# A fused attention and gated MLP on one core: six small moves in an order written out by hand

## The chip, the cores and the metric

The kernel runs on one core of one Trainium2 chip. The time is the device time of one execution in microseconds. The profile is that of one execution; all times inside it count from the start of its span.

## What is computed

Two branches read the same x (2048 rows of 1024) and are mixed by a gate of each row:

```
qkv = x @ wqkv                                  # 32 heads of 32
o   = softmax(q . k over 8 rows, 2 apart) @ v   # only rows s, s-2, ... s-14
a   = o @ wo
z   = gelu(x @ w_in);  z1, z2 = z[:, :1792], layernorm(z[:, 1792:])
g   = w_sp @ z2 + b_sp                          # mixes the 2048 rows
b   = (z1 * g) @ w_out
out = sigmoid((x * gate_w).sum(-1)) * a + (1 - sigmoid(...)) * b
```

## The kernel before

**Stages on TensorE.** (1) From 6 us: the first tiles of z2, each 8 matmuls of 448 columns (`z2_tile`, L351); then group 0 of qkv (`qkv_tile`, L724, 16 tiles of 8 matmuls of 384 columns). (2) Groups 1 to 7 of qkv, with eight z2 tiles after group 1, to 201 us; then the rest of z2. (3) z1 from about 271 us (L825): 64 tiles, each evicted by ScalarE through gelu (L827) into a staging buffer, two of them, of four tiles, stored by SP (L832). (4) The mixing by w_sp, 369 to 540 us: 16 groups `g_group(n)`, each of seven products of eight matmuls of 448 columns (L846). A group is one 2 x 2 step of Winograd's form of Strassen's product: seven products in place of eight, with sums of the operands made beforehand on VectorE (L588 to L593 for the rows of w_sp, L597 for z2), and sums of the results in PSUM, on ScalarE (`fork` L870, `keep` L856 and L858, a cast L891, L901) and on VectorE (`vec` L862). At the end of a group VectorE multiplies by z1 (L902). (5) o @ wo, 540 to about 589 us, in the same way, K of four tiles: `wo_group`, eight of them (u, two row tiles each), taken in pairs, so that product i of u and of u + 1 stand side by side. (6) y @ w_out, eight groups of seven products of 7 matmuls of 512 columns, with the final mix (`finish`, L1014, and L1091 to L1098) and the stores of the output.

The products of (4) to (6) are in f16, so their operands are scaled by powers of two taken from sums of absolute values. Rows of w_sp: L558 sums them on ScalarE, `row_power` (L562 to L565) makes the powers, `row_store` (L570 to L577) transposes them and stores them to DRAM (`rs_d`), `load_scale` (L584) reads them back for a pair of row tiles, spread over all partitions, and `scale_rows` (L588) uses them. The attention output o: `o_norm(g)` (L494) sums a head group of it on ScalarE, `o_total` (L497, L498) adds the groups up, `o_power` has TensorE add over the partitions by one matmul of 8 columns (L503) and VectorE make the powers (L504 to L509), and `heads_sums(u)` (L514 to L518) scales the rows of o for wo_group u, once `load_heads` has brought them transposed, and makes their sums. `w_scale(b)` (L985, four instructions each) scales half b of w_out.

**Attention** runs on VectorE beside stages (2) to (4): `attention_steps` yields pieces (L374 to L414) for eight head groups; ScalarE does the exponentials (L392).

**What sets the order.** The whole program is under a manual schedule: instructions stand on each engine in the order in which the Python code issues them. `Beat` keeps a planned clock: `beat.run(cols)` moves it by the columns that TensorE has been given, and issues what is due; `beat.at(t, fn)` plans fn for the time t; `vector_steps` issues attention's pieces whenever VectorE, by its own planned time, would be free. In the mixing stage three more lists are served at fixed places of a group: `beside_fork` (after L884, one entry if due), `beside_copy` (after L891, one entry if due) and `behind_mult` (after L902, entries with a planned cost, as many as fit a room of 5.0 us, of 7.4 from group 13 on). When attention is done, `attended` plans what follows, relative to the planned time t at that point: the loads of o for pairs 0 and 1, `o_total` from t + 4 on, `o_power` from t + 12 on, the scaling of wo, and `heads_sums(0)`, all by `behind_mult`; `heads_sums(1)` is appended to that list after group 13 with no earliest time.

## Time and profile before

| what | before |
|---|---|
| median of 3 runs | 678.3 us (677.97 to 679.02) |
| the profiled execution | 679.4 us |
| its span | 677.6 us |
| TensorE busy | 670.0 us (99%) |
| VectorE busy | 550.5 us (81%) |
| ScalarE busy | 394.1 us (58%) |
| granted TensorE clock | 1.00 |
| last product starts, last matmul ends | 672.45, 673.97 us |

The span runs from the first instruction to the last; the execution's time has some 1.8 us around it. PE is the matrix engine (PEld its weight loads), DVE is VectorE, ACT is ScalarE, SP the engine that issues most of the transfers; a q behind a name means the engine's instruction queue, not its unit. In the waits, "PE ps L825 <- ACT arena L827: 0.7, 1, 0.7" reads: TensorE's instructions of line 825 that write the tile ps waited for ScalarE's L827, 0.7 us in all, once, 0.7 at the longest. In the chain each line is a start, a duration and who did it, in order of time. In the timelines a line is a start, a duration, the engine, line and operation, output <- input and shapes, and in brackets the idle time just before and who ended it.

### The profile page before, as it was taken

The numbers are of one execution on the slowest core, as the hardware profiler recorded it, in microseconds if no ns is written. First come the engines' busy times: TensorE is split into PE (matmuls) and PEld (weight loads), VectorE is DVE, ScalarE is ACT, GpSimd is POOL, SyncE is SP. The second block draws the span as 40 slices with busy tenths as digits, with TensorE's granted clock in tenths as the row PEclk, the third lists the DMA queues.
The fourth block names the chain that finished last, engine by engine and source line by source line (L and its number), as shares of the span: only waits on it lengthen the run. The fifth ranks groups of instructions, "written<-read, shape, count | busy, mean of one in ns | idle before, by whom it ended". The sixth has DMA issues, their size and how long they took to land.

```text
span 677.6 us, 9538 instructions
## 1 busy us (share of the span) xinstructions
PE 670.0 (99%) x3590; PEld 392.5 (58%) x3590; DVE 550.5 (81%) x628; ACT 394.1 (58%) x736; POOL 13.1 (2%) x23
## 2 busy tenths in 40 slices
PE   9999999999999999999999999999999999999997
PEld 4577788888885555554555554555555544444443
DVE  1009799999999999999999999999957996944745
ACT  4445657565645988855983557566564664522121
POOL 1000000000000000013100000000000000000000
PEclk9999999999999999999999999999999999999999
DMA  9989769989769760527674857395769699485211
GB/s 232 178 223 236 214 176 276 239 193 270 169 170 278 266 214 3 198 73 211 231 233 137 183 135 187 108 283 133 189 208 242 128 252 252 93 177 145 58 63 62
DMA packets 230734, 123.92 MB, mean 183 GB/s; under 512 B 191008, under 2 KB 217248, under 8 KB 230688
## 3 DMA queue, kind: packets, MB, share of 16 engines
q1 hardware_dynamic: 229104, 121.21, 68.2%
q10 hardware_dynamic: 1584, 2.10, 0.9%
q8 instruction: 28, 0.46, 0.3%
q14 instruction: 18, 0.15, 0.1%
HBM read 63.97 MB, written 37.82 MB: 150 GB/s over the span
## 4 chain that ended last, share of the span: by engine, by line
PE 80%; DVE 10%; SPq 3%; DMA 3%; ACT 2%; issue 1%; ACTq 0%; DVEq 0%
PE ps L846 36%; PE ps L724 18%; PE sd L724 6%; PE seed L846 6%; PE ps L825 5%; PE ps L351 5%; DVE arena L407 2%; PE sd L825 2%; PE sd L351 2%; SPq L709 1%; DVE arena L377 1%; DVE arena L374 1%; DMA z_d<-arena 1%; DVE arena L413 1%; DMA arena<-o_d 1%
## 5 line engine op out<-in xcount | busy, mean ns | idle before, releaser
L846 PE MATMUL ps<-arena 128*128 128x448 f16 (+1 forms) x1296 | 264.8, 363 | 1.1 <-DVE arena L1014 0.6
L846 PEld LDWEIGHTS <-arena 128*128 128x128 f16 x1512 | 147.7, 98 | 156.3 <-issue 2.4
L724 PEld LDWEIGHTS <-arena 128*128 128x128 bf16 x1024 | 141.6, 138 | 25.8 <-issue 1.0
L724 PE MATMUL ps<-arena 128*128 128x384 bf16 x768 | 130.4, 326 | 0.6 <-DMA arena<-in_A_wqkv_dram 0.6
L374 DVE TENSOR_TENSOR arena<-arena 128x8192 bf16<-128x8192 bf16 x16 | 70.7, 4420 | 46.0 <-DMA arena<-k_d 45.8
L377 DVE TENSOR_TENSOR arena<-arena 128x4096 bf16<-128x4096 bf16 (+1 forms) x64 | 77.6, 1213 | 2.0
L825 PEld LDWEIGHTS <-arena 128*128 128x128 bf16 x512 | 50.0, 98 | 47.6 <-issue 1.2
L351 PEld LDWEIGHTS <-arena 128*128 128x128 bf16 x512 | 50.1, 98 | 46.7 <-issue 0.2
L351 PE MATMUL ps<-arena 128*128 128x448 bf16 (+1 forms) x384 | 77.0, 353 | 0.0
L825 PE MATMUL ps<-arena 128*128 128x448 bf16 x384 | 75.6, 352 | 0.7 <-ACT arena L827 0.7
L407 DVE TENSOR_TENSOR arena<-arena,att_A 128x8192 bf16<-128x8192 bf16 x16 | 70.7, 4421 | 0.2
L732 ACT CAST arena<-ps 128x384 bf16<-128x384 f32 x84 | 39.3, 483 | 42.3 <-PE ps L724 40.1
L846 PE MATMUL seed<-arena 128*128 128x448 f16 (+1 forms) x216 | 47.8, 363 | 0.0
L724 PE MATMUL sd<-arena 128*128 128x384 bf16 x256 | 46.8, 326 | 0.0
L827 ACT ACTIVATE arena<-ps 128x448 bf16<-128x448 f32 x48 | 24.9, 552 | 24.4 <-PE ps L825 13.7
L357 ACT ACTIVATE arena<-ps 128x448 bf16<-128x448 f32 x48 | 26.2, 550 | 21.5 <-PE ps L351 21.1
L413 DVE TENSOR_TENSOR arena<-arena 128x4096 bf16<-128x4096 bf16 x16 | 36.6, 2290 | 0.4
L1071 ACT ACTIVATE arena<-ps,omr 128x512 f32<-128x512 f32 x24 | 16.5, 688 | 32.7 <-PE ps L846 32.7
L1014 DVE SCALAR_TENSOR_TENSOR arena<-seed,omr,arena 128x512 bf16<-128x512 f32 x8 | 6.0, 751 | 34.5 <-PE seed L846 34.5
L858 ACT ACTIVATE arena<-ps,bt 128x448 f32<-128x448 f32 x32 | 20.3, 634 | 21.9 <-PE ps L846 19.8
L558 ACT ACTIVATE arena<-arena 128x2048 bf16<-128x2048 bf16 x16 | 30.7, 1922 | 0.0
L680 ACT ACTIVATE arena<-arena 128x896 bf16<-128x896 bf16 x32 | 30.2, 945 | 0.5
(144 smaller groups left out, 630.0 us busy)
## 6 DMA issues: line engine op xcount, KB each, us to landing
arena<-in_B_w_sp_dram SPq DMA_DIRECT2D x16, 512.0 KB, 4.7
arena<-k_d SPq DMA_DIRECT2D x8, 960.0 KB, 7.3
arena<-v_d SPq DMA_DIRECT2D x8, 960.0 KB, 5.9
z_d<-arena SPq DMA_DIRECT2D x16, 448.0 KB, 2.7
arena<-z_d SPq DMA_DIRECT2D x16, 448.0 KB, 4.1
y_d<-arena SPq DMA_DIRECT2D x16, 448.0 KB, 3.5
arena<-in_A_wqkv_dram SPq DMA_DIRECT2D x24, 256.0 KB, 5.6
arena<-in_B_w_in_dram SPq DMA_DIRECT2D x6, 896.0 KB, 7.9
```

Source lines behind the costliest of these rows:

```text
L351: nc.tensor.matmul(ps[:, 0:N], xT[:, kt, i * P:(i + 1) * P], w2[:, kt, ZC * c:ZC * c + N], start=(kt == 0), stop=(kt == KT - 1))
L357: nc.scalar.activation(z2[:, i, ZC * c:ZC * (c + 1)], ps[:, 0:ZC], ACT.Gelu_apprx_tanh, accum_out=s1[:, 4 * i + c:4 * i + c + 1])
L374: TT(prod.rearrange("p (w j c) -> p w j c", w=W, j=8, c=C), in0, in1, ALU.mult)
L377: return lambda: TT(pv[:, :, 0:half], pv[:, :, 0:half], pv[:, :, half:2 * half], ALU.add)
L407: TT(prod.rearrange("p (w j d h) -> p w j d h", w=W, j=8, d=DH, h=HG), in0, in1, ALU.mult)
L413: return [(4.4, mul), (2.3, lambda: TT(p3[:, 0:4, :], p3[:, 0:4, :], p3[:, 4:8, :], ALU.add)), (1.2, lambda: TT(p3[:, 0:2, :], p3[:, 0:2, ...
L558: nc.scalar.activation(waste, slot, ACT.Abs, accum_out=l1[:, a:a + 1])
L680: nc.scalar.activation(waste, g_ring[n % 4][:, r], ACT.Abs, accum_out=yl[:, k:k + 1])
L724: nc.tensor.matmul(ps[:, 0:3 * C].rearrange("p (t c) -> p t c", t=3), lhsT, wgt[:, 0:3, kt, :], start=(kt == 0), stop=(kt == KT - 1))
L732: nc.scalar.copy(st[:, j % 4, :], ps[:, 0:3 * C])
L825: nc.tensor.matmul(ps[:, 0:ZC], xT[:, kt, i * P:(i + 1) * P], w1[:, kt, :], start=(kt == 0), stop=(kt == KT - 1))
L846: nc.tensor.matmul(ps[:, 0:c1 - c0], w[:, k, :], v[:, k, c0:c1], start=(first and k == 0), stop=(k == K - 1), skip_group_check=True)
```

## The change

- `store_scale` is split off `row_store`: the store of the row scales (L577) is planned at t + 38 instead of within `row_store` at t + 20, and the first `load_scale` at t + 46 instead of t + 22.
- A tiny Exp on four columns is put into `beside_copy` ahead of the mixing stage, so that it is issued in group 0.
- `o_norm`, planned 17 us after a head group, goes to `beside_fork` if the mixing stage has begun by the time that it is due (`o_norm_soon`).
- `heads_sums(7)` is planned at +20.5 us after the first pair of wo groups instead of +17, and `w_scale(1)` at t + 30 instead of t + 31.
- z2 tile (2, 1) is issued ahead of qkv group 0 instead of after qkv.
- The last product of the last group is issued as two halves of 256 columns, each followed by its `finish` and its store.

```diff
                 else:
-                    beat.at(t + 17.0, lambda g=g: o_norm(g - 1, obuf))
+                    beat.at(t + 17.0, lambda g=g: o_norm_soon(g - 1))
...
+    def o_norm_soon(g):
+        if prep["mixing"]:
+            beside_fork.append((0.0, lambda: o_norm(g, obuf)))
+        else:
+            o_norm(g, obuf)
+
...
         beat.on_vector(0.8)
+
+    def store_scale():
         sync.dma_start(rs_d.rearrange("(a t) -> a t", t=P), rs_r[:])
...
         z2_tile(i, 0)
+    z2_tile(2, 1)
     beat.steps = vector_steps(beat.now + NJ * KT * 3 * C * BEAT + 8.0)
...
     for i in range(16):
-        for c in range(1 if i > 1 else 2, 4):
+        for c in range(1 if i > 2 else 2, 4):
             z2_tile(i, c)
...
     beat.at(t + 20.0, row_store)
-    beat.at(t + 22.0, lambda: load_scale(0))
+    beat.at(t + 38.0, store_scale)
+    beat.at(t + 46.0, lambda: load_scale(0))
...
+    beside_copy.append((0.0, lambda: nc.scalar.activation(wsc[:, 3:4], cm05[:, 0:1], ACT.Exp)))
     for m in range(11):
         beside_copy.append((beat.now + 10.0, lambda m=m: wo_norm(m)))
...
-    beat.at(t + 31.0, lambda: w_scale(1))
+    beat.at(t + 30.0, lambda: w_scale(1))
...
-            plan_heads(7, beat.now + 0.3, 1.5, beat.now + 17.0)
+            plan_heads(7, beat.now + 0.3, 1.5, beat.now + 20.5)
...
-        product(pa, v.a22, e4, 0, 512, False)
-        finish(o21, pa, hi, m21)
         if u == NU - 1:
             sync.dma_start(out2[(2 * u + 1) * P:(2 * u + 2) * P, 512:D], o22)
-            sync.dma_start(out2[(2 * u + 1) * P:(2 * u + 2) * P, 0:512], o21)
+            for c0 in (0, 256):
+                sl = slice(c0, c0 + 256)
+                for k in range(NF // 2):
+                    nc.tensor.matmul(pa[:, sl], v.a22[:, k, :], e4[:, k, sl], start=False,
+                                     stop=(k == NF // 2 - 1), skip_group_check=True)
+                nc.vector.scalar_tensor_tensor(o21[:, sl], pa[:, sl], hi, m21[:, sl], ALU.mult, ALU.add)
+                sync.dma_start(out2[(2 * u + 1) * P:(2 * u + 2) * P, sl], o21[:, sl])
         else:
+            product(pa, v.a22, e4, 0, 512, False)
+            finish(o21, pa, hi, m21)
             sync.dma_start(out2[(2 * u + 1) * P:(2 * u + 2) * P, :], ob_slots[2 * u + 1])
```

## The prediction

> **What bounds the kernel now.** I read the page's first two parts, then the waits of TensorE, then the chain of work that ended last around each of those waits, then the timelines of VectorE and TensorE where the built order of the changed kernel differs.

> ```profile
> PE 670.0 (99%) x3590; PEld 392.5 (58%) x3590; DVE 550.5 (81%) x628; ACT 394.1 (58%) x736; POOL 13.1 (2%) x23
> ...
> PE   9999999999999999999999999999999999999997
> ...
> DVE  1009799999999999999999999999957996944745
> ```

> TensorE is busy for 670.0 of 677.6 us, in every slice. VectorE is nearly full only in the slices up to 500 us. So the end moves only by what stands between two matmuls, and by the tail behind the last one. All such gaps together are small:

> ```profile
> PE ps L825 <- ACT arena L827: 0.7, 1, 0.7
> PE ps L724 <- DMA arena<-in_A_wqkv_dram: 0.6, 1, 0.6
> PE ps L846 <- DVE arena L1014: 0.6, 1, 0.6
> PE ps L846 <- ACT arena L858: 0.5, 1, 0.5
> ```

> These are idle times. Measured from matmul start to matmul start against the usual spacing, the trace gives 0.79 us at 22.08, 0.91 and 0.12 at 321.74 and 326.40, 0.18 at 386.24, 0.64 at 411.10, 0.12 at 547.67, 0.22 at 551.35 and 0.74 at 575.39: 3.72 us. More than this cannot be won ahead of the tail. The chain says what each of them waited for:

> ```profile
> 16.90 5.05 DMA arena<-in_A_wqkv_dram
> ```
> ```profile
> 302.20 4.27 SPq L584
> ...
> 308.57 6.81 DMA z_d<-arena
> ```
> ```profile
> 406.77 1.28 ACT L392
> ```
> ```profile
> 564.22 5.63 DMA arena<-o_d
> ...
> 573.40 1.27 DVE arena L985 x2
> 574.68 0.67 DVE arena L1014
> ```

> **The parts that remove a wait.** *One more z2 tile first.* The eight matmuls are only moved (one z2 tile takes 1.51 us, row L351). The weights land at 21.95 and TensorE would now come to L724 at 21.29 + 1.51 = 22.80. The whole 0.79 goes: **-0.79**. The tile's inputs are those of the tiles beside it; what is late next is nothing in this stretch.

> *Row scales stored later.* L577 had to wait for VectorE until 300.93, and the load L584 right behind it, which reads what L577 wrote, held SP's queue for 4.27 us. Behind them stood the z1 stores L832 (306.57 and 308.57), so ScalarE had no staging buffer for L827, and TensorE no free bank. In the built order L577 stands behind the next z1 stores and L584 later still, when the store has long landed, so neither should hold the queue. **-1.03** (0.91 + 0.12). Bounds 0 (SP is held again, at another place) and -1.03. Nothing on SP waits for the two in between: the scales are first read by L588 at 340.11, and the load is planned some 20 us before.

> *Exp table in group 0.* At 411.10 the path was: L858 ends 406.75, table load 1.28, Exp 0.63 (row L392), L891, L654, u3's L858. Without the load ScalarE is 1.28 earlier there, more than the 0.64: **-0.6** (bounds -0.64 and 0, since in the built order Exp, L654 and L650 still stand ahead of that L858). The load moves to group 0: L891 ends at 376.20, load 1.28, a tiny Exp of about 0.21 (as the smallest activation row, L621), then L858 of 0.63 ends near 378.35; the last product that waits for it starts at 378.5. Cover 0.15: cost 0, and 0.1 to 0.5 if the tiny Exp takes as long as the real one.
> [...]

> *o_norm* beside a fork: L494 (1.92) no longer stands between L856 and L858 of group 1: **-0.18**.

> *Last o pair (heads 7) later.* At 575.39 L514 of heads 7 waited for its transfer until 569.95, and L985 x4 and L1014 queued behind it. In the built order L985 x8 come first, then L1014, heads 7 (L514 to L518, 2.26), L1014 x2. TensorE's a22 of group 5 needs the second L1014: from the end of s3 of group 4, 0.1 + 0.67 + 2.26 + 0.75 = 3.78, while four products of 0.866 take 3.46. A stall of 0.32 to 0.4 replaces 0.74: **-0.35** (bounds -0.74 and 0).

> **What the same edits move elsewhere.** The order of the kernel comes from a planned clock, so attention's last pieces slide. In the built order the last L410 stands behind L902 of group 11 (it stood ahead of it), its o_norm in group 12, and two things follow one group later.

> ```profile
> 508.84 1.09 DVE L902 TENSOR_TENSOR arena<-arena 128x1792 bf16<-128x1792 bf16 x1 [1.55 <-ACT arena L901]
> 509.85 0.15 DVE L497 TENSOR_REDUCE wsc<-both 128x1 f32<-128x8 f32 x1
> 510.04 0.23 DVE L498 TENSOR_SCALAR rs_n<-both,wsc 128x8 bf16<-128x8 f32 x1
> ```
> ```profile
> 518.57 0.17 PE L503 MATMUL ps<-rs_n,zeros 128*128 128x8 bf16 x1
> ```
> ```profile
> 535.83 0.74 DVE L514 TENSOR_SCALAR arena<-arena,var 128x2048 f16<-128x2048 bf16 x1
> ...
> 541.37 1.09 DVE L902 TENSOR_TENSOR arena<-arena 128x1792 bf16<-128x1792 bf16 x1
> 542.38 0.75 DVE L514 TENSOR_SCALAR arena<-arena,var 128x2048 f16<-128x2048 bf16 x1
> ```

> *o_total behind group 13.* L497 and L498 stood behind L902 of group 12, 8 us ahead of L503, so L503 (0.17) waited for nothing. Now they stand behind L902 of group 13, and L503 still stands on TensorE between groups 13 and 14. So TensorE ends group 13 and waits for L901 (start +0.08, 0.64), L902 (+1.01 to the next instruction), L497 (+0.19), L498 (0.23) and some 0.04 to 0.2 of semaphores: 2.2 to 2.4. **+2.35**. Behind L503 stands the whole of group 14. It cannot be hidden, since L902 of a group needs that group's last product.

> *Sums of heads 1 behind group 15.* L514 of heads 1 ran at 535.83, ahead of L902 of group 15. Now it comes right behind that L902. TensorE's second wo product (a11 of heads 1) reads what L514 writes. From the end of group 15: L901 to +0.72, L902 +1.01, L514 0.75, semaphores 0.05: 2.53, and only the first wo product (0.866) lies beside it: 1.67. VectorE comes to L902 late besides: L902 of group 14, heads 0 (2.26), L529 x4 (4.7), y scale (2.05) and L862 x2 end some 0.36 after L901. **+2.03** (bounds 1.67 and 2.4).

> *Two halves.* The last product becomes 2 x 7 matmuls of 256 columns, 0.757 each by columns. In the built order the second half's first matmul waits for VectorE's L1014 of the first. With L1014 at 0.45 for half the columns (0.75 for 512; the smallest VectorE row is 0.15): 0.757 + 0.04 + 0.45 + 0.04 + 0.757 + 0.04 + 0.45 = 2.53, against 1.515 + 0.04 + 0.75 = 2.30: +0.23. The last store is 64 KB instead of 128 KB; 256 and 128 KB land in 2.1 and 2.0 us, so -0.05. **+0.2**. Bounds -0.25 (halves overlap) and +0.9 (seven more weight loads of 98 ns that nothing hides).
> [...]

> **Sum.** -0.79 - 1.03 - 0.6 - 0.18 - 0.35 = -2.95; +2.35 + 2.03 + 0.2 = +4.58; together +1.6, with 0.1 for small waits that move: **+1.7**. The profiled execution took 679.4 us (span 677.6), so 681.1 there. The median is 678.3, 1.1 under it: **680.0 us**.

> **Rivals.**
> *Nothing replaces the waits:* L498 is done before group 13's last product and heads 1 before the first wo product, as now. Then -3.72 and the tail: 678.3 - 3.6 = 674.7, faster. It turns on one thing, whether L498 still waits for L902 of group 13; the built order says it does. 0.06.
> *Gains full, new waits least:* -3.72 + 2.2 + 1.67 - 0.25 = -0.1: 678.2. For it: each wait that goes is named by the chain; against it: the heads 7 order leaves 0.3. 0.13.
> *The early gains are lost:* VectorE is 90% busy and more up to 500 us; if the mixing stage waits for it, TensorE gives back the 1.8 us that it won before 368: 681.8. For: the row of nines. Against: TensorE shows no wait for VectorE there now. 0.13.
> [...] 0.08.
> *The forecast:* 0.60.

> Within 0.2% (1.36 us, 676.9 to 679.7) is about what a measurement of this kernel cannot tell from no change. The forecast's own spread, 679.2 to 681.0 by its bounds, lies about seven tenths above 679.7. Slower: 0.42 + 0.13 + 0.08 = 0.63; same: 0.18 + 0.13 = 0.31; faster: 0.06. The range 678.2 to 681.6 leaves out the first rival and part of the third.

> **What would show it.** TensorE has no wait for in_A_wqkv and none for L827; ACT's table load stands at about 376; TensorE waits some 2.2 us ahead of the 8-column matmul of L503 for VectorE's L498, and some 2 us ahead of the second wo product for L514. If either of these is under 1 us, the forecast is wrong, and the time lies near 678 or under. A wait of TensorE for L902 or L588 in the mixing stage would speak for the third rival.

## The result, and the profile after

The changed kernel takes 682.9 us (median of 6, 681.7 to 684.9) against 678.7 for before in the same comparison (677.9 to 679.4): a ratio of 1.0066, 95% interval 1.0047 to 1.0085. It is slower, as forecast, but by 4.3 us (682.94 - 678.66) where 1.7 was forecast, and above the range. Line numbers of the changed kernel are 6 to 11 higher behind the first edits: L503 has become L509, L498 L504, L514 L520, L846 L856, L902 L912, L1014 L1025.

TensorE's waits in the profile after (engine, line, releaser: us in all, times, longest):

```profile
PE ps L856 <- DVE arena L520: 2.3, 1, 2.3
PE ps L509 <- DVE rs_n L504: 2.2, 1, 2.2
...
```

The waits for in_A_wqkv, for L827 and for the Exp are gone. Behind 20 us the list has only two more: 0.6 us between the two halves of the last product (L1117) and 0.4 for L1025. Two new waits of over 2 us stand in the place of those that went, where the built order had shown them. The chain of work ahead of the first (start, duration, who):

```profile
513.96 2.09 PE ps L856 x11
516.06 0.03 issue
516.08 0.64 ACT arena L911
516.72 0.05 issue
516.77 1.09 DVE arena L912
517.87 0.08 DVE wsc L503
517.95 0.03 issue
517.97 0.24 DVE rs_n L504
518.21 0.04 issue
518.26 0.17 PE ps L509
```

What the forecast does not have is in the table by stretches of the same profile, each 3.41 us long (stretch, length, then for PE, PEld, DVE, ACT and POOL the busy us with the count of instructions, the granted clock, the DMA engines' share and GB/s):

```profile
514.67:518.08 3.41, 1.38 (x8) 0.59 (x6) 3.28 (x8) 1.66 (x3) 0.00 (x0) 1.00 1.36 324
518.08:521.49 3.41, 3.23 (x10) 1.34 (x10) 3.05 (x10) 0.02 (x1) 0.00 (x0) 0.50 0.96 272
521.49:524.90 3.41, 3.41 (x19) 1.76 (x18) 0.48 (x1) 1.44 (x3) 0.00 (x0) 1.00 1.32 238
541.97:545.38 3.41, 1.12 (x6) 0.51 (x6) 3.29 (x6) 0.57 (x1) 0.00 (x0) 1.00 1.04 312
545.38:548.79 3.41, 3.41 (x9) 1.21 (x8) 3.31 (x8) 1.34 (x3) 0.00 (x0) 0.50 1.00 191
548.79:552.20 3.41, 3.41 (x17) 1.57 (x16) 1.52 (x4) 3.02 (x5) 0.00 (x0) 1.00 0.99 184
```

Around the end of each wait (518.26 and 544.34) the granted clock falls to 0.50 for 3.41 us (by the trace's records of it from 518.06 and from 545.37). TensorE is all but full there and gets 9 or 10 matmuls done instead of 17 to 19. A 448-column matmul starts 0.37 us after the one before instead of 0.19. By start-to-start times that is 1.56 us lost behind the first wait and 1.69 behind the second, together more than a third such wait would cost, in a place where the list of waits shows nothing.

By the same measure, in us, against the first profile of before (spans 683.1 and 677.6, +5.5):

| term | forecast | these two profiles |
|---|---|---|
| wait for in_A_wqkv | -0.79 | -0.79 |
| wait for L827 | -1.03 | -1.03 |
| Exp table at 411 (0.15 left) | -0.6 | -0.49 |
| o_norm | -0.18 | -0.18 |
| heads 7 (0.53 left) | -0.35 | -0.21 |
| o_total behind group 13 | +2.35 | +2.38 |
| heads 1 behind group 15 | +2.03 | +2.45 |
| tail in halves | +0.2 | +0.30 |
| half rate behind the two waits | 0 | +3.2 |
| sum | +1.6 | +5.6 |

### The profile page after: what moved, and what is told of

It is laid out like the page before. It is cut to its first block, busy times and chain, and to the rows that moved or that the text cites. A ratio compares the mean times of both kernels' runs of the same rounds, so it can differ in the third digit from the quotient of the medians.

```text
span 683.1 us, 9553 instructions
## 1 busy us (share of the span) xinstructions
PE 673.1 (99%) x3597; PEld 394.1 (58%) x3597; DVE 550.9 (81%) x629; ACT 394.8 (58%) x737; POOL 8.5 (1%) x23
## 4 chain that ended last, share of the span: by engine, by line
PE 96%; DVE 1%; DMA 1%; ACT 0%; issue 0%; SPq 0%; DVEq 0%
PE ps L856 37%; PE ps L732 18%; PE ps L351 11%; PE ps L835 11%; PE seed L856 6%; PE sd L732 6%; PE sd L351 4%; PE sd L835 4%; DVE arena L1025 0%; DMA arena<-in_A_x_dram 0%; DMA y_d<-arena 0%; ACT arena L688 0%; PE pt L334 0%; DVE arena L520 0%; DVE arena L702 0%
## 5 line engine op out<-in xcount | busy, mean ns | idle before, releaser
L856 PE MATMUL ps<-arena 128*128 128x448 f16 (+1 forms) x1289 | 266.8, 366 | 2.7 <-DVE arena L520 2.3
L856 PEld LDWEIGHTS <-arena 128*128 128x128 f16 x1505 | 147.8, 98 | 161.9 <-issue 8.2
L351 PEld LDWEIGHTS <-arena 128*128 128x128 bf16 x512 | 50.1, 98 | 46.6 <-issue 0.2
L351 PE MATMUL ps<-arena 128*128 128x448 bf16 (+1 forms) x384 | 76.5, 353 | 0.0
L856 PE MATMUL seed<-arena 128*128 128x448 f16 (+1 forms) x216 | 47.8, 363 | 0.0
L837 ACT ACTIVATE arena<-ps 128x448 bf16<-128x448 f32 x48 | 25.4, 551 | 21.5 <-PE ps L835 20.5
L1025 DVE SCALAR_TENSOR_TENSOR arena<-seed,omr,arena 128x512 bf16<-128x512 f32 x8 | 6.0, 751 | 34.4 <-PE seed L856 34.4
```

The source lines that it names most:

```text
L351: nc.tensor.matmul(ps[:, 0:N], xT[:, kt, i * P:(i + 1) * P], w2[:, kt, ZC * c:ZC * c + N], start=(kt == 0), stop=(kt == KT - 1))
L856: nc.tensor.matmul(ps[:, 0:c1 - c0], w[:, k, :], v[:, k, c0:c1], start=(first and k == 0), stop=(k == K - 1), skip_group_check=True)
```

## Experiments

**Theory.** The z2 tile, issued ahead of qkv, moves the planned start of attention by one tile (1.51 us). That is enough for attention's last piece to miss a group, so `o_total` and the sums of heads 1 come one group late; TensorE waits twice, and each wait can bring half rate behind it. **Rivals:** another edit does it (o_norm, Exp); the slow matmuls have another cause than the wait, such as the transposed loads of o beside them.

**The changed kernel without its z2 tile.** Edit:

```diff
-    z2_tile(2, 1)
...
-        for c in range(1 if i > 2 else 2, 4):
+        for c in range(1 if i > 1 else 2, 4):
```

> The changed kernel without its z2 tile ahead of qkv; the other five edits stay. Theory 1 (the z2 tile moves attention's plan by one tile, that puts o_total behind group 13 and the sums of heads 1 behind group 15, and the two waits of TensorE that follow, with the half-rate matmuls behind each, are the whole loss): no wait ahead of the 8-column matmul, none ahead of the second wo product, no matmul at 0.37 us for 448 columns; the wait for in_A_wqkv of 0.79 is back; about 1 us under before (677.5), and all executions at one time. Rival (the loss comes from the other five edits, o_norm or the Exp above all): the waits and the slow matmuls stay, 682 to 684.

Measured: 678.0 (677.3 to 678.6), ratio 0.9991 (0.9983 to 1.0000). No wait for L504, none for L520, clock 1.00. The wait for in_A_wqkv came back with 0.46 in its profile, and at 391 us TensorE waits 0.2 us for one of VectorE's sums of the rows of w_sp (L600 here). The other five edits are not the loss.

**All six edits, attention's plan put back.** The loads keep their time; only the steps on VectorE are planned 1.51 us earlier:

```diff
         beat.at(t - 7.9, lambda: load_v(0))
+        t -= KT * ZC * BEAT
```

> The changed kernel with all six edits, but attention's plan starts one z2 tile (1.51 us) earlier, as it stood before. Theory 1: as the run without the z2 tile, less the 0.79 us of the wait for in_A_wqkv: about 676.8, faster than before by some 0.25%. Rival (the tile itself costs something, by its place ahead of qkv): as slow as the changed kernel, or no faster than the run without the tile.

Measured: 676.8 (676.3 to 677.2), ratio 0.9973 (0.9963 to 0.9983): faster than both kernels. VectorE's timeline has the sum of o behind group 12 again (L913 is L902, L504 and L505 are L497 and L498):

```profile
506.15 1.09 DVE L913 TENSOR_TENSOR arena<-arena 128x1792 bf16<-128x1792 bf16 x1 [1.55 <-ACT arena L912]
507.16 0.15 DVE L504 TENSOR_REDUCE wsc<-both 128x1 f32<-128x8 f32 x1
507.35 0.23 DVE L505 TENSOR_SCALAR rs_n<-both,wsc 128x8 bf16<-128x8 f32 x1
```

The tile costs nothing by itself. The plan that starts behind it does.

**Before with the z2 tile alone.**

> Before with the z2 tile alone. Theory 1: the wait of 0.79 goes, both new waits come (2.4 and 2.45), and in some executions one or two stretches of half-rate matmuls of 1.6 to 1.8 us each: 682 to 686, about 1 us slower than the changed kernel, with its spread. Rival: within 0.2% of before.

Measured: 684.4 (682.6 to 686.1), ratio 1.0083 (1.0068 to 1.0097). Its waits:

```profile
PE ps L847 <- DVE arena L514: 2.3, 1, 2.3
PE ps L503 <- DVE rs_n L498: 2.2, 1, 2.2
PE ps L847 <- ACT arena L859: 1.7, 2, 1.3
```

One moved tile brings both waits. The third line is that of Exp and o_norm (the other edits take it away): with attention shifted it is 1.43 and 0.59 by start-to-start times instead of 0.64 and 0.18. In this profile half rate followed the first wait only (521.79 to 525.20). The second wait, 2.29 us long, had none (PE alone: busy us and count, clock, DMA share and GB/s):

```profile
542.27:545.68 3.41, 2.16 (x11) 1.00 0.79 238
545.68:549.09 3.41, 2.37 (x11) 1.00 1.05 256
```

**The changed kernel, TensorE kept busy.** Ahead of L509, and ahead of the second wo product:

```diff
+        for _ in range(9):
+            nc.tensor.matmul(ps[:], ident[:], mask[:], start=True, stop=True)
         nc.tensor.matmul(ps[:, 0:NU], ones, ol_n[:, 0:NU], start=True, stop=True)
```

> The changed kernel with nine matmuls of 512 columns of constants (about 1.95 us) ahead of the 8-column matmul and as many ahead of the second wo product, so that TensorE does something while it waits; they add to no result. The clock theory (an idle stretch of over 2 us makes the granted clock fall to half for some 3.3 us): both waits shrink to about 0.3 us, no matmul behind them is at half rate, clock 1.00 in all executions, 681 us with the spread of before. Rival (the matmuls behind are slow for another reason, such as the transposed loads of o that run at the same time, or the waits themselves end later): the matmuls behind still take 0.37 us, 683 to 685.

Measured: 681.8 (681.1 to 682.3), ratio 1.0046 (1.0034 to 1.0058). The waits shrank to 0.3 each, and the stretches behind them run at full clock beside the same loads:

```profile
518.00:521.40 3.40, 3.40 (x20) 1.75 (x19) 3.30 (x9) 0.99 (x2) 0.00 (x0) 1.00 1.11 329
...
542.30:545.70 3.40, 3.40 (x16) 1.57 (x17) 3.30 (x9) 1.87 (x3) 0.00 (x0) 1.00 1.00 204
```

So in this run the half rate went with the idleness, and the loads alone did not bring it; the mean clock was 0.999 or 1.000 in all five executions. The two waits themselves still cost what they cost: 681.76 is 4.9 above the 676.82 of the version with the plan put back, and the two waits were 2.38 + 2.45.

**Idle stretches of chosen lengths**, in before's z1 stage (the second run has the six counts of copies in the other order):

```diff
+            rest = dict(zip((5, 15, 25, 35, 45, 55), (2, 4, 6, 8, 11, 15))).get(16 * c + i)
+            if rest:
+                for _ in range(rest):
+                    nc.scalar.copy(ones, z1s[:, i % 4, 0:P])
+                pw = psum.tile([P, 512], F32, name="pw", tag="ps")
+                nc.tensor.matmul(pw[:, 0:8], ident[:], ones[:, 0:8], start=True, stop=True)
```

> Before, with six idle stretches of TensorE put into the z1 stage, 15 us apart: behind z1 tiles 5, 15, 25, 35, 45, 55 ScalarE makes 2, 4, 6, 8, 11, 15 small copies of what it has just evicted, and one matmul of 8 columns on their result (used by nothing) holds TensorE. By the rows of L827 (0.55) and some 0.2 us a copy the idle stretches are about 1.0, 1.4, 1.8, 2.2, 2.8 and 3.6 us. Clock theory: no slow matmuls behind 1.0 (before has 0.75 without), 3.3 us of half rate behind the two longest, and the limit lies between; each costs 1.6 to 1.8 us whatever the idle length. Rival 1: half rate lasts as long as the idle did. Rival 2 (no matter of idleness): no slow matmul at all.

> The same with the six lengths in the other order, 15, 11, 8, 6, 4, 2 copies. If a limit of idle time alone decides, the same lengths are followed by half rate as in the other run. If the place in a window of fixed length decides too (the half-rate stretches begin a whole number of windows of 3.3 to 3.4 us apart), the middle lengths, 1.4 to 2.2 us, may differ between the two runs, and the longest and shortest do not.

Measured: 717 and 714 us, two executions each. The lengths did not come out as planned, since other work stood in ScalarE's queue: 2.55 to 6.78 us in the one run, 1.35 to 7.92 in the other. Of the twelve, 1.35 and 2.59 had no half rate behind them; the ten others had, the shortest of them 2.55. So the length alone did not decide it here. Here is the time of the run in rising order, divided into cells of 3.41 us that start where the clock changes (columns as above):

```profile
283.30:286.71 3.41, 2.89 (x9) 0.50 0.02 5
...
300.36:303.78 3.42, 0.87 (x6) 1.00 0.42 98
303.78:307.19 3.41, 3.41 (x11) 0.50 1.01 280
...
368.63:372.04 3.41, 1.95 (x7) 0.50 0.00 0
372.04:375.46 3.42, 3.42 (x11) 0.50 0.00 0
```

And of the run in falling order:

```profile
352.25:355.67 3.42, 0.51 (x4) 1.00 0.97 382
355.67:359.08 3.41, 3.41 (x11) 0.50 1.00 342
...
369.32:372.73 3.41, 2.84 (x16) 1.00 0.94 283
372.73:376.15 3.42, 1.39 (x9) 1.00 0.27 92
```

A step of 3.41 us fits each run: in the first the half-rate stretches end at 286.71, 307.19, 331.08, 351.56, 375.46 and 399.35, which are 6, 7, 6, 7 and 7 times 3.41 us apart, in the second at 290.81, 314.71, 338.60 and 359.08, 7, 7 and 6 times. In each cell of these two runs, of the z2-alone run and of the changed kernel that was read so, the clock is 1.00 or 0.50, and it went with how busy TensorE was in the cell before. At full clock, the twelve cells with 0 to 1.28 us busy were followed by half rate; cells with 2.06 or more were not; at 1.39 one was (the changed kernel, 514.66 to 518.08) and one was not (the last line above). That cell holds 2.02 us of the idle stretch of 2.59, and the cell before it the rest. What decides between 1.28 and 2.06 is not shown. At half clock a cell with 2.89 us busy was followed by full clock, and those with 1.78, 1.95 and 2.28 by another half cell. So neither rival holds: half rate lasted 3.41 or 6.83 us behind idle stretches of 2.55 to 7.92, and idleness that an edit put in brought it in ten of twelve places.

The second wait of the z2-alone run agrees with this. A cell ended at 545.68, inside the wait, so that 1.25 us of idleness fell into the one cell and the rest into the next. It also fits the spread of the changed kernel's executions: 681.7 to 682.2 with a mean clock of 0.999, 683.7 and 684.0 with 0.997, and 684.9, the profiled one, with 0.994. One cell at half rate takes 0.0025 off the mean (1.71 us of 683), so these would be none, one and two cells behind the two waits. Only one of the six was profiled, so for the others this is argued from the mean alone. It is not the whole spread: one execution of the z2-alone run took 684.8 us at a mean clock of 1.000, another 682.6.

**Two matmuls of the nine.**

> The changed kernel with two matmuls of 512 columns of constants (0.43 us) ahead of each of the two waits, where the kept-busy run had nine. They add to no result. The idle stretches become 1.8 to 1.9 us. In the runs so far half rate followed where over 2.0 us of idleness fell into one window of 3.41 us, and not where 1.25 did. If that limit holds, no half-rate matmul in any execution: 681.7 and clock 1.00 as in the kept-busy run, though TensorE waits almost as long as in the changed kernel. Rival (the limit lies lower, or the two matmuls are too few): some executions 1.6 to 3.2 us longer, 682 to 685.

Measured: 681.5 to 681.8 in four executions, median 681.7, ratio 1.0046 (1.0032 to 1.0059). A fifth execution, the profiled one, took 1842.9 us at a mean clock of 1.000. Why is not known; it is left out, and with it the only profile. In the four others the mean clock was 0.999 or 1.000, and their times are the changed kernel's lowest, without its higher ones. That 0.43 us of work in each wait of 2.2 is enough is not shown by this: three of the changed kernel's own six executions had no cell at half rate by their mean clock, so that four of four can be chance.

**One last product.** The version with the plan put back, its last product whole:

> All edits with attention's plan put back, but the last product whole, with one store, as before. The account of the tail (halves: a wait of 0.74 between the halves, the last store 0.44 earlier) says 0.3 us faster than with halves, 676.5. Rival (the halves are worth something by the shorter last store): 0.2 to 0.5 slower, 677.1.

Measured: 676.5 (676.1 to 676.8), ratio 0.9962 (0.9948 to 0.9976). In the profile of before, with one product, the end comes 3.62 us after the last matmul, in that of the changed kernel, with halves, 3.18, and the halves have a wait of 0.74 between them: 0.3 in favour of one product. The medians differ by as much, but the executions overlap.

**Before once more.**

> Before once more, for a second profile, since the first one is of an execution 0.7 us above the median. Theory (the waits of TensorE differ from one execution to the next, and those of the first profile are larger than the usual): a span of 676 to 677 us, with less than 3.72 us of waits behind 20 us. Rival (what differs lies in other places, the start or the rate of matmuls): the same waits, 3.6 to 3.8 us.

Measured: 678.5 (677.3 to 679.4); the profiled execution has a span of 676.1, 1.5 less than the first profile of the same kernel. Its waits:

```profile
PE ps L825 <- ACT arena L827: 0.5, 1, 0.5
PE ps L846 <- ACT arena L858: 0.5, 1, 0.5
```

The lines for in_A_wqkv and for L1014 are not there. Start to start the gaps behind 20 us sum to 2.1 us, not 3.7: 0.11 at the first qkv tile instead of 0.79, 0.67 at 321 instead of 0.91, none at 575 (L514 of heads 7 started at 568.03, not 569.95). Those three hang on when a transfer lands, and that differs between these two profiles. The Exp and o_norm gaps, which hang on the order alone, are the same 0.64 and 0.18.

**Heads 7.** As in before (the first kernel), and later, at +22.0 (the second), both on the version with one last product:

> The version with attention's plan put back, one last product, and heads 7 and the second w_scale as in before (so: z2 tile, row scales, Exp, o_norm). In the second profile of before the wait at 575 us was not there, since the transfer of o landed 1.9 us earlier; the changed order has 0.53 there in every profile. Theory: the edit costs 0.5 in the usual execution and saves 0.2 in the late one; without it 676.0 to 676.3, against 676.5 with it. Rival: the late transfer is the usual one, 676.8.

> The same, but heads 7 planned at +22.0 us (and the second w_scale at +30), so that its sums stand behind three of the four L1014 of the pair of groups 4 and 5. Both products of a22 then find their L1014 done: no wait there in any execution, 676.0, the fastest of all, 0.4% under before. Rival (the sums of heads 7 are then late for the last pair): a wait of up to 1 us at about 576, 676.5 to 677.5.

Measured: 676.1 (675.6 to 677.6), ratio 0.9965 (0.9952 to 0.9979), and 676.4 (675.8 to 677.2), ratio 0.9968 (0.9956 to 0.9981). With before's order the wait at 573 us is 1.52 in its profile, of an execution of 677.2. With heads 7 later it is gone, but that profile has 0.68 for in_A_wqkv in spite of the tile, since TensorE came there at 22.99 and the weights later still. The three versions cannot be told apart by these runs, so neither expectation is settled. Any of them is 0.3 to 0.4% faster than before.

## Why the prediction was right in sign and wrong in size

- **The waits that go:** right in mechanism, each term within 0.15 us of the profile it was read from. The load of the table in group 0 cost nothing, as forecast: the cast L901 ends at 374.18, the load takes 1.28 from 374.20, the tiny Exp 0.20 from 375.49. The next activation starts 0.01 us after the load, and TensorE has no wait there. The 0.08 among the chances is for a stop of ScalarE longer than the load, which no run shows.
- **o_total behind group 13:** right, 2.35 forecast, 2.38 measured. **Heads 1:** right, with a size of 2.03 instead of 2.45. VectorE came to L902 of group 15 1.34 us after the group's end, where the sum had 1.08 (0.72 + 0.36). At 2.45 it lies just above its bounds of 1.67 to 2.4. **Halves:** +0.3, forecast +0.2.
- **The step that failed: the two new waits were priced as waits alone.** "What the same edits move elsewhere" has each wait's length and nothing for what stands behind it, and no rival had it. The runs put half-rate matmuls there: 1.56 and 1.69 us in the profiled execution, and 682.94 - 681.76 = 1.2 between the medians with and without idleness. It was not readable from the profile of before, whose waits behind 20 us are all under 0.8 us and whose clock is 1.00. Only the first matmuls of the kernel hint at a slower clock (L114 from 1.59 us: 512 columns in 0.43 us, as behind the second wait, instead of 0.22); the trace has no record of the clock before 6.35 us.
- **The second step that failed: the conversion to the median.** The gains were read from an execution 1.1 us above the median, and then 1.1 was subtracted for it. But, as far as two profiles show, the surplus of that execution lies in the very waits that the change takes away (3.7 us of gaps against 2.1 in the second profile, whose span is 1.5 shorter), so the full gains do not hold against the median. Against the median the six edits together win 1.8 us without the new waits (678.66 - 676.82), not 2.75.
- **The sum again:** -1.8 + 4.8 + 1.2 = +4.2; measured +4.3. The -1.8 and the 1.2 are differences of these same medians, so what the sum checks is the 4.8 from the trace: between the version kept busy and the one with the plan put back it is 4.9. The forecast was -2.75 + 4.38 + 0.1 = +1.7.
- The rival by which VectorE would take back the early gains did not come: the changed kernel's waits have none for L902 or L588 (now L912 and L596) in the mixing stage, and neither has the version with the plan put back. The run without the z2 tile has one for VectorE there, of 0.2 us, so the mixing stage is not far from it.

## What to carry to other kernels

Where an order comes from a planned clock, an instruction moved in one stage moves the plan of every stage that starts from that clock; compare the built order of all engines, not only around the edit, and put the plan's start back if the real start has not moved. TensorE's waits of 2.2 and 2.3 us cost 1.56 and 1.69 us beyond their length here, at a granted clock of 0.50: look at the clock in the stretch behind a wait, and fill the wait with matmuls on constants if it can't be removed (nine kept the clock at 1.00 here). A gain that is read from one profile holds for that execution; waits that end with a transfer differed between the two profiles of before (0.79 and 0.11 us at the first qkv tile), so take a second profile before adding them up.
